# Subtracting the mean on ScalarE instead of VectorE in a banded-attention and MLP kernel, with two weight sums moved

## The chip, the cores and the metric

The kernel runs on one core of one Trainium2 chip. The metric is the device time of one execution in microseconds (us). Medians, with lowest and highest, are over all executions of a kernel that were timed. The profile is one traced execution. Its span is about 1.7 us shorter than the time that the same execution is given, so spans are compared with spans and times with times.

## The reference, cut to what matters

```python
# q, k, v: (8 batches, 8 heads, 576 positions, 64); window of 64 positions
scores = where(0 <= i - j < 64, q @ k.T / 8, -1e9)
x  = (softmax(scores) @ v).transpose(0, 2, 1, 3).reshape(8, 576, 512)
mu, var = mean(x), mean((x - mu) ** 2)              # of each row of 512
xn = (x - mu) / sqrt(var + 1e-6) * g_ln
out = x + relu(xn @ w_ch1) @ w_ch2                  # 512 -> 2048 -> 512
```

## The kernel before

Rows are worked in nine groups of 512, each of four blocks of 128 rows (`kb`). Groups 0 to 7 are the first 512 positions of each batch; group 8 collects the last 64 of all batches. For every block `b_step` multiplies scores by V, divides by the softmax sum, and takes mean and variance. `z_step` makes the f16 rows for the MLP, `zt_step` transposes them on TensorE and copies the result to `zT` on ScalarE. In groups 0 and 1 `z` is only `x - mean`; the division by the standard deviation is done at the end, in `add_out`, because ReLU lets a positive factor through.

```python
def b_step(g, kb):
    ...                                             # xps = attention product on TensorE
    nc.vector.reciprocal(out=rcp, in_=xps[:, :, D])                             # L323
    nc.vector.tensor_tensor(out=xn, in0=xps[:, :, 0:D], in1=rcp_b, op=ALU.mult) # L326
    nc.vector.bn_stats(out=stats, in_=xv)                                       # L328
    nc.vector.bn_aggr(out=mvg[g][:, kb, :], in_=stats)                          # L331
    if g < 2:
        z_step(g, kb)

def z_step(g, kb):
    z = p_blk.tile([128, DM], FP16, tag="z", ...)
    ...
    if g < 2:
        nc.vector.tensor_scalar(out=z, in0=xv, scalar1=mu, scalar2=None, op0=ALU.subtract)  # L341
        return
    ...                                             # groups 2 to 8: on GpSimd

def zt_step(g, kb, eng="act"):
    ...                                             # from group XZ on: a DMA transposes, most blocks
    for kc in range(NKC):
        nc.tensor.transpose(out=ztp[:, kc, :], in_=z[:, 128*kc:128*(kc+1)], identity=ident16)
    nc.scalar.copy(out=dst, in_=ztp)                # L363

def l1_half(half, i):                               # half a group of the first layer, two banks' worth
    ...                                             # matmuls hph (L531)
    nc.scalar.activation(out=hrT[...], in_=hps, func=AF.Relu, bias=0.0, scale=1.0)          # L536
```

A plan says in which slot of which group's MLP each of these steps is emitted. In program order the plan reads as follows (cut):

```python
zt_step(0, 0); vB_cur(0, 3, 0)
b_step(0, 2)                     # ends in z_step(0, 2)
zt_step(0, 1)                    # its copy gives zT to the first half of the first layer
s_mm(0, 3, True)                 # scores and exp of block 3
...
if g == 0:
    at(0, b_step, 0, 3); at(1, zt_step, 0, 2); at(3, zt_step, 0, 3); at(4, newton, 0, 0, 4)
    ...
    at(18, b_step, 1, 0); at(21, b_step, 1, 1); at(22, zt_step, 1, 0); at(24, zt_step, 1, 1)
    ...
    at(33, b_step, 1, 2)
if g == 1:
    ...
    at(1, b_step, 1, 3); at(2, zt_step, 1, 2); at(5, zt_step, 1, 3)
    at(25, w2_sums, 3, 0, 4); at(28, w2_sums, 3, 4, 8)     # T3 = b22 - b12
    ...
if g == 2:                                                 # T2 = T3 + b11, then T1 and T4
    for m, i in enumerate((2, 1, 4)):
        at(4 + 2*m, w2_sums, i, 0, 4); at(5 + 2*m, w2_sums, i, 4, 8)
```

The softmax here doesn't subtract the row's maximum and nothing guards it: scores larger than these inputs give would overflow.

## Time and profile before

| | before |
|---|---|
| time, median of the first three runs (lowest to highest) | 311.75 us (311.21 to 312.38) |
| profiled span | 310.4 us |
| mean granted TensorE clock | 0.998 |
| TensorE's last matmul ends / the output stores then take | 304.8 / 5.7 us |

The busy shares, the chain that ended last and the timelines of the start and of the seam between groups 0 and 1 are in the prediction.

### The profile page before, as it was taken

The page shows a single profiled execution, that of the slowest core. Times are in us where ns is not written, and L with a number is a line of the kernel's source. Part 1 is how long each engine was busy: PE and PEld are TensorE (multiplying, and loading weights), DVE is VectorE, ACT ScalarE, POOL GpSimd, SP SyncE. Part 2 cuts the span into 40 slices and gives each one's busy share as a digit, 9 for nine tenths or more (in the row PEclk, how much of TensorE's full clock was granted, in tenths as well). Part 3 has the DMA queues.
Part 4 walks back from the last instruction along what each step waited for, and adds up shares of the span by engine and source line. Part 5 has one row for each costly group of instructions (what it writes and reads, how often), then busy time and mean ns, then how long its engine had stood idle before and what let it go on. Part 6 is the DMA issues. An engine that isn't in the chain of part 4 may idle for free.

```text
span 310.4 us, 7624 instructions
## 1 busy us (share of the span) xinstructions
PE 297.7 (96%) x3089; PEld 197.6 (64%) x3089; DVE 222.0 (72%) x411; ACT 153.0 (49%) x258; POOL 172.2 (55%) x255
## 2 busy tenths in 40 slices
PE   7988998999999999999999999999999999999992
PEld 4556544597454468646964686459646855788882
DVE  0779585775775996589666965896569685777972
ACT  2586633487326742776247626762375048315500
POOL 6669676563871798279815983698246506204300
PEclk9999999999999999999999999999999999999999
DMA  8999999999766995899179997993690393003013
GB/s 193 259 385 291 334 356 278 291 297 185 163 166 193 255 196 116 259 298 138 35 224 309 202 159 219 312 146 66 205 179 19 52 203 137 2 0 137 0 37 101
DMA packets 109893, 57.43 MB, mean 185 GB/s; under 512 B 79841, under 2 KB 100833, under 8 KB 109858
## 3 DMA queue, kind: packets, MB, share of 16 engines
q1 hardware_dynamic: 108800, 53.75, 69.9%
q0 software_dynamic: 768, 2.80, 3.8%
q8 instruction: 24, 0.39, 0.5%
q10 hardware_dynamic: 290, 0.40, 0.4%
q14 instruction: 11, 0.09, 0.1%
HBM read 38.80 MB, written 9.44 MB: 155 GB/s over the span
## 4 chain that ended last, share of the span: by engine, by line
PE 81%; DVE 7%; SPq 4%; DMA 3%; ACT 1%; POOL 1%; issue 1%; POOLq 0%; ACTq 0%
PE hps L395 28%; PE pA L472 11%; PE pB L472 7%; PE pC L472 7%; PE hph L531 6%; PE ch L407 6%; PE xps L320 4%; PE sc L286 3%; DMA w1s<-in_moe_w_ch_dram 3%; PE tp L229 2%; PE lA L581 2%; SPq L141 2%; DVE sS L446 2%; PE ch L546 1%; SPq L89 1%; PE lC L581 1%
## 5 line engine op out<-in xcount | busy, mean ns | idle before, releaser
L395 PE MATMUL hps<-zT,w1g 128*128 128x512 f16 x416 | 96.3, 380 | 0.0
L399 ACT ACTIVATE hrT<-hps 128x512 f16<-128x512 f32 x104 | 62.4, 600 | 38.6 <-PE hps L395 35.0
L395 PEld LDWEIGHTS <-w1g 128*128 128x128 f16 x416 | 38.3, 98 | 41.9 <-issue 0.9
L293 ACT ACTIVATE pt<-sc 128x512 f16<-128x512 f32 x72 | 39.0, 595 | 27.8 <-DVE xn L479 15.6
L472 PEld LDWEIGHTS <-sS 128*128 128x128 f16 x448 | 43.3, 98 | 5.4 <-issue 0.5
L345 POOL TENSOR_SCALAR rsz<-mvg 128x1 f32<-128x1 f32 x28 | 10.3, 370 | 59.6 <-DVE mvg L331 58.6
L128 POOL CAST qk<-qk 128x1024 f16<-128x1024 f32 x32 | 35.6, 1128 | 13.7 <-DMA qk<-in_q_dram 8.3
L472 PEld LDWEIGHTS <-hrT 128*128 128x128 f16 x336 | 32.5, 98 | 5.3 <-ACT hrT L620 0.3
L215 ACT COPY qkT<-tp 128x1024 f16<-128x1024 f16 x16 | 16.1, 1012 | 35.9 <-PE tp L229 26.7
L300 DVE TENSOR_TENSOR pt<-pt,mask 128x1024 f16<-128x1024 f16 x32 | 25.6, 805 | 9.6 <-ACT pt L293 9.6
L479 DVE TENSOR_TENSOR xn<-pA,xn 128x512 f32<-128x512 f32 x28 | 19.2, 686 | 17.2 <-PE pA L472 17.2
L472 PE MATMUL pA<-wT,sS 128*128 128x256 f16 x224 | 26.9, 273 | 0.3 <-DVE xn L479 0.3
L348 POOL TENSOR_SCALAR z<-xn,rsz 128x512 f16<-128x512 f32 x28 | 25.3, 904 | 2.9
L472 PE MATMUL pC<-w2s,sS 128*128 128x256 f16 x224 | 26.9, 273 | 0.0
L323 DVE RECIPROCAL rcp<-xps 128x8 f32<-128x8 f32 x36 | 7.4, 205 | 26.1 <-PE xps L320 25.9
L328 DVE BATCH_NORM_STATS2 stats<-xn 128x6 f32<-128x512 f32 x36 | 25.0, 695 | 1.2
L326 DVE TENSOR_TENSOR xn<-xps,rcp 128x512 f32<-128x512 f32 x36 | 24.9, 691 | 1.2
L531 PE MATMUL hph<-zT,w1g 128*128 128x256 f16 x192 | 23.9, 273 | 1.8 <-ACT zT L363 1.1
L446 DVE TENSOR_TENSOR sS<-hrT 128x512 f16<-128x512 f16 (+1 forms) x40 | 24.5, 613 | 0.6 <-ACT hrT L399 0.6
L407 PE MATMUL ch<-w2s,hrT 128*128 128x512 f16 x96 | 22.9, 380 | 0.3 <-DVE xn L417 0.3
L531 PEld LDWEIGHTS <-w1g 128*128 128x128 f16 x192 | 17.9, 98 | 5.1 <-issue 1.5
L320 PEld LDWEIGHTS <-pt 128*64 128x64 f16 x576 | 12.2, 110 | 13.7 <-issue 5.9
(109 smaller groups left out, 454.1 us busy)
## 6 DMA issues: line engine op xcount, KB each, us to landing
out_dram<-xn SPq DMA_DIRECT2D x33, 256.0 KB, 2.7
qk<-in_q_dram SPq DMA_DIRECT2D x16, 512.0 KB, 6.4
qk<-in_k_dram SPq DMA_DIRECT2D x16, 512.0 KB, 7.4
v<-in_v_dram SPq DMA_DIRECT2D x32, 256.0 KB, 6.3
w2s<-in_moe_w_ch_dram SPq DMA_DIRECT2D x9, 512.0 KB, 9.0
w1s<-in_moe_w_ch_dram SPq DMA_DIRECT2D x4, 512.0 KB, 7.3
tk<-in_k_dram SPq DMA_DIRECT2D x8, 256.0 KB, 4.6
tv<-in_v_dram SPq DMA_DIRECT2D x8, 256.0 KB, 5.2
```

The costliest lines, as they stand in the source:

```text
L128: nc.gpsimd.tensor_copy(out=dst[:, :].rearrange("p (a j) e d -> p a e j d", j=j), in_=t[:, :].rearrange("p (a e j d) -> p a e j d", e=2, j ...
L293: nc.scalar.activation(out=o, in_=i, func=AF.Exp, bias=0.0, scale=scale)
L300: nc.vector.tensor_tensor(out=ptv, in0=ptv, in1=mb, op=ALU.mult)
L326: nc.vector.tensor_tensor(out=xn, in0=xps[:, :, 0:D], in1=rcp_b, op=ALU.mult)
L328: nc.vector.bn_stats(out=stats, in_=xv)
L348: nc.gpsimd.tensor_scalar(out=z, in0=xv, scalar1=rs, scalar2=nm, op0=ALU.mult, op1=ALU.add)
L395: nc.tensor.matmul(out=hps, lhsT=w1g[:, kc, 128 * hc:128 * (hc + 1)], rhs=zT[g][:, kc, :], start=(kc == 0), stop=(kc == NKC - 1),)
L399: nc.scalar.activation(out=hrT[:, hc, :], in_=hps, func=AF.Relu, bias=0.0, scale=1.0)
L407: nc.tensor.matmul(out=ch[kb], lhsT=hrT[:, hc, 128 * kb:128 * (kb + 1)], rhs=w2s[:, hc, :], start=(hc == 0), stop=(hc == NHC - 1),)
L446: nc.vector.tensor_tensor(out=o, in0=x, in1=y, op=op)
L472: nc.tensor.matmul(out=o, lhsT=a[:, c, 128 * p:128 * p + 128], rhs=wv[:, c, :], start=(first and (p == 0 or split_c) and c == 0), stop=(c ...
L531: nc.tensor.matmul(out=hps[:, e], lhsT=w1g[:, kc, 128 * hc:128 * (hc + 1)], rhs=zT[g][:, kc, 256 * half:256 * half + 256], start=(kc == 0) ...
```

## The change

Its intent is to take six of the eight subtractions of groups 0 and 1 off VectorE, where they collide with GpSimd's casts (the worst took 1885 ns instead of 486). ScalarE computes `Identity(x + bias)` with the bias minus the mean, which VectorE prepares as a 128x1 negation. The transpose of block 1 of group 1 comes one unit later, which gives `z` more time. The sum T3 of W2 comes earlier in group 1 and T2 takes its old slots there, a group sooner than before, which frees VectorE early in group 2. Whole diff:

```diff
@@ z_step
         if g < 2:
-            nc.vector.tensor_scalar(out=z, in0=xv, scalar1=mu, scalar2=None, op0=ALU.subtract)
+            if g == 0 and kb < 2:
+                nc.vector.tensor_scalar(out=z, in0=xv, scalar1=mu, scalar2=None, op0=ALU.subtract)
+            else:
+                nmu = p_blk.tile([128, 3], FP32, tag="rsz", name=f"nmu_{g}_{kb}")[:, 0:1]
+                nc.vector.tensor_scalar(out=nmu, in0=mu, scalar1=-1.0, scalar2=None, op0=ALU.mult)
+                nc.scalar.activation(out=z, in_=xv, func=AF.Identity, bias=nmu, scale=1.0)
             return
@@ plan, g == 0
-            at(24, zt_step, 1, 1)
+            at(25, zt_step, 1, 1)
@@ plan, g == 1
-            at(25, w2_sums, 3, 0, 4)
-            at(28, w2_sums, 3, 4, 8)
+            at(7, w2_sums, 3, 0, 4)
+            at(8, w2_sums, 3, 4, 8)
+            at(25, w2_sums, 2, 0, 4)
+            at(28, w2_sums, 2, 4, 8)
@@ plan, g == 2
-            for m, i in enumerate((2, 1, 4)):
+            for m, i in enumerate((1, 4)):
```

## The prediction

> **What bounds the kernel now.** I read the page first (busy shares, then the chain that ended last), then the timeline of single stretches, and in it the start of each matmul against the start of the one before.
>
> ```profile
> PE 297.7 (96%) x3089; PEld 197.6 (64%) x3089; DVE 222.0 (72%) x411; ACT 153.0 (49%) x258; POOL 172.2 (55%) x255
> PE 81%; DVE 7%; SPq 4%; DMA 3%; ACT 1%; POOL 1%; issue 1%; POOLq 0%; ACTq 0%
> ```
>
> TensorE is busy for 96%, and 81% of the chain that ended last is its own work. VectorE, which the change relieves, is 7% of it. Busy alone would not prove that TensorE has no slack, so I looked at the starts: from 26.7 us on, matmuls of 256 columns start every 0.11 us and those of 512 every 0.22. Larger holes than a normal change of weights are few: 0.2 us at 39.8, 0.2 at 46.3, 0.8 at 48.4, 0.4 at 49.1, 0.4 at 59.85, 0.5 at 116.0, 0.4 at 120.4, and none above 0.2 after that. So whatever TensorE loses before about 120 us reaches the end almost whole, and the most that this change can win is what it removes of those holes.
>
> The start, where blocks 2 and 3 of group 0 (rows in blocks of 128) are made (timeline, all engines; start, length, engine, line, tiles, idle before):
>
> ```profile
> 19.56 0.59 ACT L363 COPY zT<-ztp 128x512 f16<-128x512 f16 x1
> 20.04 1.09 ACT L293 ACTIVATE pt<-sc 128x512 f16<-128x512 f32 x2
> 20.20 1.27 PE L531 MATMUL hph<-zT,w1g 128*128 128x256 f16 x8 [0.21 <-ACT zT L363]
> 20.63 0.18 DVE L331 BATCH_NORM_AGGREGATE mvg<-stats 128x2 f32<-128x6 f32 x1
> 20.85 0.49 DVE L341 TENSOR_SCALAR z<-xn,mvg 128x512 f16<-128x512 f32 x1
> ...
> 23.58 0.18 DVE L331 BATCH_NORM_AGGREGATE mvg<-stats 128x2 f32<-128x6 f32 x1
> 25.58 0.60 ACT L536 ACTIVATE hrT<-hph 128x512 f16<-128x512 f32 x1 [0.28 <-PE hph L531]
> 26.08 0.58 ACT L363 COPY zT<-ztp 128x512 f16<-128x512 f16 x1
> 26.71 3.65 PE L531 MATMUL hph<-zT,w1g 128*128 128x256 f16 x32 [0.94 <-ACT zT L363]
> ```
>
> ScalarE copies zT of block 1 before the mean of block 2 exists (20.81), and TensorE starts the MLP at once.
>
> The seam between groups 0 and 1 (same view):
>
> ```profile
> 47.05 1.33 DVE L341 TENSOR_SCALAR z<-xn,mvg 128x512 f16<-128x512 f32 x1
> 47.06 1.04 POOL L128 CAST qk<-qk 128x1024 f16<-128x1024 f32 x1 [0.78 <-PE ch L546]
> 48.31 1.39 DVE L417 SCALAR_TENSOR_TENSOR xn<-ch,rstdg,xn 128x512 f32<-128x512 f32 x2
> 48.44 0.40 PE L360 MATMUL ztp<-ident,z 128*128 128x128 f16 x4 [0.65 <-DVE z L341]
> 49.10 1.89 PE L407 MATMUL ch<-w2s,hrT 128*128 128x512 f16 x8 [0.26 <-DVE xn L417]
> ...
> 59.71 0.60 ACT L536 ACTIVATE hrT<-hph 128x512 f16<-128x512 f32 x1 [2.12 <-PE hph L531]
> 61.20 1.05 PE L531 MATMUL hph<-zT,w1g 128*128 128x256 f16 x8
> 61.40 0.18 DVE L331 BATCH_NORM_AGGREGATE mvg<-stats 128x2 f32<-128x6 f32 x1
> ```
>
> At 47 us a 0.49 us subtraction takes 1.33 beside a GpSimd cast, and TensorE waits for it: this is what the change aims at. At 59.71 ScalarE empties the first hph bank before the mean of block 2 of group 1 exists (61.58).
>
> **What the Trainium skill says.** "SBUF — State Buffer", Who interferes with whom: VectorE's two-port operations (copy, cast, tensor_scalar) and GpSimd's instructions exclude each other for a whole instruction, while ScalarE waits for nobody. The trace agrees: the eight subtractions have a median of 486 ns and a maximum of 1885. It also shows that tiny ones are caught: the 128x4 steps of newton take 0.16 us alone and 0.63 beside GpSimd's w1 casts. "ScalarE: Activation LUTs", What ACT_TABLE_LOAD costs: an ACTIVATE with a pointer bias takes 280 ns + 0.833 ns per element, 707 ns for 512; the trace has no such row named, its ACTIVATEs of 512 take 600. I use 0.62 to 0.70. Both orders have one table load only, so Identity costs none. "TensorE: Matmul & The Clock Gate", Part 1: the array falls to half speed after an idle window of some 3.4 us. The trace shows two speeds at the start (transposes every 0.107 us until 8.7, then every 0.056).
>
> **The change part by part.** Built orders of both kernels show three moves.
>
> (a) Six subtractions (0.49 alone) leave VectorE; six 128x1 negations (0.16 alone, an estimate from newton's 128x4 rows) come, so 6 x 0.33 = 2.0 us less VectorE work. Six Identity passes, about 3.9 us, go to ScalarE, which is at 49%. Neither total bounds the kernel; what counts is that ScalarE works in order, and the new pass stands where the block step is written, in front of work that was ready earlier.
>
> Group 0, block 2: the pass comes ahead of the zT copy of block 1. Mean ready 20.81, negation to 21.01, pass 21.07 to 21.69, zT copy 21.6 to 22.2 (was 20.15), exps of block 3 to 23.2 (were 21.13). First hph at 22.25, 2.05 late. Block 3: attention product at 23.27 instead of 21.39; from there to its mean takes 2.37 us as before, so 25.64; the negation, in the middle of back-to-back casts, ends about 26.2; pass to 26.85. It stands before the ReLU of the second hph bank, which then ends at 27.4 and frees the bank of the fourth hph: 27.45 to 28.3; ReLU, then zT of block 3 to 29.5 (was 26.66). The second half of hph starts at 29.5 in place of 26.71: **+2.8 us**, less 0.2 because w2's last cast (46.28) is then no longer waited for.
>
> Group 1, blocks 0 and 1: ScalarE is idle from 41.7 to 46.3, so both passes fit. The wait for z goes, and the transpose a unit later gives it 0.86 us more. But the next matmul still needs the bank that the add at L417 frees, which runs after the mean of block 1 (47.02) and the negation: 48.0 to 48.7 by the clock of before, depending on whether a cast catches the negation. TensorE stood at 49.96 after that unit and the transpose; it will at 49.1 to 49.85. **-0.4 us**.
>
> Group 1, block 2: the pass now stands before the ReLU of the first hph. With TensorE 2.6 us later, GpSimd's casts of q and k at 56 to 58.6 are over when VectorE masks, so that mask is 0.7 shorter and 0.4 of hole at 59.85 goes. Mean at about 61.0, negation to 61.2, pass to 61.9, ReLU to 62.4: the third hph starts 62.45 instead of 61.20. Block 3: mean 63.1, pass to 63.95, ReLU of the third bank to 64.45, just in time. Sum **+1.3 us** (already net of the 0.4); if the cast of v catches this last negation it is up to 1.9 more.
>
> (b) T3 moves to the time after the qkT copies of group 1, where VectorE is idle for 3.0 us; T2 takes T3's old slots (same shape). So 2 x 0.68 us leave the stretch at 100 to 102 us of group 2, and the two halves of T4 move ahead of block 1's reciprocal. VectorE is full from 103 to 116, and TensorE waits at its end:
>
> ```profile
> 100.36 1.29 DVE L712 TENSOR_TENSOR wT<-wT,w2s 128x1024 f16<-128x1024 f16 x2
> 104.92 0.66 DVE L712 TENSOR_TENSOR wT<-w2s,wT 128x1024 f16<-128x1024 f16 x1
> 115.29 0.69 DVE L479 TENSOR_TENSOR xn<-pA,xn 128x512 f32<-128x512 f32 x1
> 116.03 1.91 PE L472 MATMUL pA<-wT,sS 128*128 128x256 f16 x16 [0.34 <-DVE xn L479]
> ```
>
> With some 1.3 us less in that stretch the hole of 0.5 closes, and perhaps part of the 0.4 at 120.4: **-0.6 us**.
>
> Sum: 2.8 - 0.2 - 0.4 + 1.3 - 0.6 = +2.9, so 311.75 + 2.9 = 314.6.
>
> **Rivals.** First, the change does what it is for: ScalarE has room, VectorE's collisions go, and the blocking is absorbed because the start waits for weights. Then only the gains stay, 0.4 + 0.4 + 0.6 and part of the 0.8, some 1.5 us: 310.2. For it speaks that the MLP waits for w1 casts at 23.28 and 23.95; against it that in my times the ReLU behind block 3's pass, not w1, is last by more than 3 us. Second, VectorE's negations are as exposed to GpSimd as the subtractions were, and each sits on the path to a ScalarE pass on which others queue: with the 1.9 of group 1 and another 0.5 in group 0 the time is 317. Third, TensorE's pauses at the start (2.3 us before the first hph, 1.7 before the fourth) come close enough to an idle window to drop its clock; some 3 us at half speed add 1.5 to 3 us: 316 to 318. The pauses of 0.9 us in the trace of before did not do so.
>
> **Range and chances.** My blocking terms follow from fixed orders and measured lengths; uncertain are the collisions with GpSimd, about 1.5 us either way, and whether I missed an absorption. 8 in 10: 311.0 to 317.5. Two per cent slower means over 318.0, which needs the second and third rivals together: 0.08. Two per cent faster means under 305.5, more than all holes after 26.7 us: 0.01.
>
> **What would show it.** First hph near 22.3 us and second half near 29.5; on ScalarE zT of block 1 after the pass; TensorE waiting for the ReLU at the third hph of group 1; no wait for z at the late transpose; the hole at 116 gone. If the second half starts before 27.5, the prediction is wrong by its main term; if it starts near 29.5 and the end is not later, something after it had slack that I did not see.

## More of the kernel before

One more view is useful for comparing: what TensorE itself waited for in the kernel before (columns: who waited for whom, us in total, times, the longest).

```profile
PE hph L531 <- ACT zT L363: 1.1, 2, 0.9
...
PE ztp L360 <- DVE z L341: 0.6, 1, 0.6
...
PE pA L472 <- DVE xn L479: 0.3, 1, 0.3
```

The whole list is some 6 us long in an execution of 310. The wait for `z` is the one that the change aims at; the wait of `pA` is the one that the moved sums may close.

## The result, and the profile after

| | before | after |
|---|---|---|
| time, median (lowest to highest), 6 runs each | 311.48 us (311.02 to 312.38) | 315.14 us (314.93 to 316.3) |
| ratio of the fast runs, 95% interval | | 1.0119 (1.0098 to 1.0141) |
| profiled span | 310.4 | 313.6 |
| mean granted TensorE clock | 0.998 | 0.989 |
| VectorE / ScalarE busy | 222.0 / 153.0 | 218.4 / 156.4 |

A ratio here and below is the mean time of one kernel's fast runs over that of the other's of the same rounds, so it is not quite the ratio of the medians that are quoted. Executions over 1.5% slower than the fastest of the same kernel are left out of the means. The changed kernel is 1.2% slower, well outside the scatter. The prediction was 314.6.

The line of the page on the chain that ended last, changed kernel:

```profile
PE 87%; ACT 5%; DVE 5%; issue 1%; POOL 0%; POOLq 0%; ACTq 0%
```

ScalarE went from 1% of that chain to 5%, VectorE from 7% to 5%. What TensorE waited for, changed kernel:

```profile
PE hph L536 <- ACT zT L368: 3.1, 2, 2.2
...
PE hph L536 <- ACT hrT L541: 1.5, 1, 1.5
```

Line numbers moved by up to five (L531 became L536). The waits for `z` and for the add before `pA` have left the list. In their place the wait of `hph` for the copy of `zT` grew from 1.1 to 3.1 us, and one of 1.5 us for a ReLU is new: both releasers are on ScalarE.

The start of group 0, changed kernel, timeline (start, length, engine, line, operation, idle before):

```profile
21.03 0.15 DVE L345 TENSOR_SCALAR nmu<-mvg 128x1 f32<-128x1 f32 x1
21.22 0.72 ACT L346 ACTIVATE z<-xn,nmu 128x512 f16<-128x512 f32 x1 [1.50 <-DVE nmu L345]
21.85 0.57 ACT L368 COPY zT<-ztp 128x512 f16<-128x512 f16 x1
22.46 1.15 PE L536 MATMUL hph<-zT,w1g 128*128 128x256 f16 x8 [2.19 <-ACT zT L368]
24.12 1.89 PE L536 MATMUL hph<-zT,w1g 128*128 128x256 f16 x8
26.34 0.72 ACT L346 ACTIVATE z<-xn,nmu 128x512 f16<-128x512 f32 x1 [2.09 <-DVE nmu L345]
26.96 0.58 ACT L541 ACTIVATE hrT<-hph 128x512 f16<-128x512 f32 x1
...
29.79 2.45 PE L536 MATMUL hph<-zT,w1g 128*128 128x256 f16 x21 [0.94 <-ACT zT L368]
```

The order on ScalarE: the pass for block 2 at 21.22, after an idle time of 1.50 us, and only then the copy of `zT` of block 1, which stood at 19.56 before. TensorE starts the MLP at 22.46 instead of 20.20. The same happens with block 3 at 26.34, ahead of a ReLU. The second half of `hph` starts at 29.79 instead of 26.71.

Block 2 of group 1, same view:

```profile
63.19 0.72 ACT L346 ACTIVATE z<-xn,nmu 128x512 f16<-128x512 f32 x1 [3.52 <-DVE nmu L345]
63.82 1.06 ACT L541 ACTIVATE hrT<-hph 128x512 f16<-128x512 f32 x2
64.45 1.03 PE L536 MATMUL hph<-zT,w1g 128*128 128x256 f16 x8 [1.50 <-ACT hrT L541]
```

ScalarE stood idle for 3.52 us in front of the pass, and the ReLU that would have emptied a bank stood behind it.

Following one and the same matmul through both traces gives the ledger, in us. Each row is the start of that matmul; the third column is the running difference, the fourth what the stretch since the row above added. (Both spans start 0.19 apart already at 17 us.)

| matmul | before | after | late by | added | predicted |
|---|---|---|---|---|---|
| first `hph` of group 0 | 20.20 | 22.46 | 2.26 | 2.07 | 2.05 |
| second half of `hph` | 26.71 | 29.79 | 3.08 | 0.82 | 0.75 |
| `ch` after the last cast of W2 | 46.34 | 49.37 | 3.03 | -0.05 | -0.2 |
| first layer's end, after the seam | 49.96 | 52.09 | 2.13 | -0.90 | -0.4 |
| third `hph` of group 1 | 61.20 | 64.45 | 3.25 | 1.12 | 1.3 with the rest of the stretch |
| `pA` with wT | 116.03 | 118.66 | 2.63 | -0.62 | -0.6 |
| end of TensorE | 304.79 | 307.41 | 2.62 | -0.01 | 0 |
| end of the span | 310.45 | 313.57 | 3.12 | 0.50 | 0 |

### The profile page after: what moved, and what is told of

It is laid out like the page before. It is cut to its first block, busy times and chain, and to the rows that moved or that the text cites. A ratio compares the mean times of both kernels' runs of the same rounds, so it can differ in the third digit from the quotient of the medians.

```text
span 313.6 us, 7634 instructions
## 1 busy us (share of the span) xinstructions
PE 298.2 (95%) x3089; PEld 199.1 (63%) x3089; DVE 218.4 (70%) x411; ACT 156.4 (50%) x264; POOL 171.1 (55%) x255
## 4 chain that ended last, share of the span: by engine, by line
PE 87%; ACT 5%; DVE 5%; issue 1%; POOL 0%; POOLq 0%; ACTq 0%
PE hps L400 30%; PE pA L477 12%; PE pB L477 8%; PE pC L477 8%; PE ch L412 6%; PE hph L536 6%; PE sc L286 4%; PE xps L320 4%; PE tp L229 3%; ACT pt L293 2%; PE lA L586 2%; PE warm L749 1%; DVE stats L328 1%; PE lC L586 1%; DVE xn L326 1%; ACT qkT L215 1%
## 5 line engine op out<-in xcount | busy, mean ns | idle before, releaser
L400 PEld LDWEIGHTS <-w1g 128*128 128x128 f16 x416 | 38.3, 98 | 42.0 <-issue 0.9
L300 DVE TENSOR_TENSOR pt<-pt,mask 128x1024 f16<-128x1024 f16 x32 | 26.6, 838 | 6.9 <-ACT pt L293 6.7
L536 PE MATMUL hph<-zT,w1g 128*128 128x256 f16 x192 | 24.6, 281 | 4.7 <-ACT zT L368 3.1
L536 PEld LDWEIGHTS <-w1g 128*128 128x128 f16 x192 | 18.6, 100 | 7.8 <-issue 2.8
```

Source lines behind the costliest of these rows:

```text
L300: nc.vector.tensor_tensor(out=ptv, in0=ptv, in1=mb, op=ALU.mult)
L400: nc.tensor.matmul(out=hps, lhsT=w1g[:, kc, 128 * hc:128 * (hc + 1)], rhs=zT[g][:, kc, :], start=(kc == 0), stop=(kc == NKC - 1),)
L536: nc.tensor.matmul(out=hps[:, e], lhsT=w1g[:, kc, 128 * hc:128 * (hc + 1)], rhs=zT[g][:, kc, 256 * half:256 * half + 256], start=(kc == 0) ...
```

## The experiments

Three theories were on trial. **Order**: ScalarE works in order, and the pass, which must wait for its mean, stands in front of work that is ready; what costs is the wait, not the work. **Work**: the passes themselves, or the longer path mean, negation, pass, cost the time. **Clock**: the pause of TensorE at the start dropped its clock. The last is not idle: in the timeline above, the eight matmuls at 24.12 took 1.89 us, which is half speed. Twelve kernels were run, in three calls; each call has its own runs of the kernel before on the same chip: 312.14 (310.68 to 315.6), 312.19 (311.0 to 312.92) and 311.68 (310.71 to 315.19), 11 runs each. All twelve gave correct results.

### a4_late_pass: the same passes, issued later

The changed kernel's instructions, with four of the six passes issued behind the work that is ready first. VectorE's order stays as it is.

```diff
-                nc.scalar.activation(out=z, in_=xv, func=AF.Identity, bias=nmu, scale=1.0)
+                late[(g, kb)] = (z, xv, nmu)      # z_pass(g, kb) issues the activation
+                if g == 1 and kb < 2:
+                    z_pass(g, kb)
...
 s_mm(0, 3, True)
+z_pass(0, 2)
...
 at(1, zt_step, 0, 2)
+at(1, z_pass, 0, 3)
...
+at(1, z_pass, 1, 2)       # group 1, before b_step(1, 3)
+at(3, z_pass, 1, 3)       # group 1
```

> The changed kernel with the same instructions, VectorE's order untouched; only four of the six ScalarE passes are issued later (group 0 block 2 after the exps of block 3, group 0 block 3 after the zT copy of block 2, group 1 block 2 after the second ReLU, group 1 block 3 after the fourth). Theory O (the loss is ready work of ScalarE standing behind a pass that waits for its mean): the 2.9 us of group 0 and the 1.1 us of group 1 go, the gains of the seam (0.9) and of the sums (0.5) stay: 310.1 us, 0.986 of the changed kernel. Rival W (the passes and negations cost by their work or by the longer path mean, negation, pass, transpose): nothing changes, 315 us. Rival C (the clock that fell to half between 24 and 26 us): nothing is changed in the cause either, unless the hole goes; then as O.

312.47 us (311.7 to 314.69), ratio 1.0023 (0.9983 to 1.0064): no longer distinguishable from the kernel before, though not the gain that I had expected. Timeline of this kernel at the start of group 0:

```profile
21.58 1.03 PE L544 MATMUL hph<-zT,w1g 128*128 128x256 f16 x8 [0.21 <-ACT zT L376]
...
22.42 0.72 ACT L361 ACTIVATE z<-xn,nmu 128x512 f16<-128x512 f32 x1
...
27.36 3.65 PE L544 MATMUL hph<-zT,w1g 128*128 128x256 f16 x32 [1.04 <-ACT zT L376]
```

The pass of 0.72 us is still there, but beside TensorE's work, and `hph` waits 0.21 us instead of 2.19. (This execution began 1.4 us late, hence 21.58; by 49 us that was made up.) At 116 us TensorE is 0.98 ahead of the kernel before. So in this trace the passes as work cost TensorE nothing. The end is another matter: the output stores took 6.31 us instead of 5.66 (see "Not foreseen" below), which takes back most of what TensorE won. Two of the six runs took 314.5 and 314.7; they were not traced and I cannot explain them, but runs like these occur in the kernel before too (314.18 and 315.6, the latter counted as slow).

### a5_tiny_read: the wait without the work

The kernel before, with the subtraction left on VectorE, plus a ScalarE instruction on one column that reads the mean at the place where the pass would stand. Its result is not used.

```diff
             nc.vector.tensor_scalar(out=z, in0=xv, scalar1=mu, ..., op0=ALU.subtract)
+            if not (g == 0 and kb < 2):
+                tiny = p_blk.tile([128, 3], FP32, tag="rsz", name=...)[:, 0:1]
+                nc.scalar.activation(out=tiny, in_=mu, func=AF.Identity, bias=0.0, scale=1.0)
```

> The kernel before, subtractions still on VectorE, no negations; at the place of each of the six passes ScalarE copies 128x1 of the mean into a scratch tile nobody reads. Theory O: the wait alone costs, so most of the loss appears without its work: mean of group 0 block 2 at 20.8, zT copy of block 1 to 21.7 instead of 20.15; second ReLU behind the mean of block 3; +1.3 us in group 0 and +1.2 in group 1: 314.0 us (1.008 of before). Rival W: six operations of 0.2 us on an engine half idle, within 0.3 us of before: 311.6.

314.88 us (313.91 to 317.29), ratio 1.0095 (1.0057 to 1.0133). Timeline of this kernel:

```profile
21.11 0.20 ACT L344 ACTIVATE tiny<-mvg 128x1 f32<-128x1 f32 x1 [1.31 <-DVE mvg L331]
21.22 0.57 ACT L366 COPY zT<-ztp 128x512 f16<-128x512 f16 x1
21.84 1.03 PE L534 MATMUL hph<-zT,w1g 128*128 128x256 f16 x8 [1.54 <-ACT zT L366]
```

Six instructions of 0.20 us, 1.2 us of work in all on an engine that is half idle, cost most of what the change cost. The copy that the MLP needs begins at 21.22, once the tiny read has had its mean, instead of 19.56. This refutes the theory of work and shows that the wait in the wrong place is enough. My sizes: +1.3 for group 0, and the trace has 1.43 (28.14 against 26.71); +1.2 for group 1, which was too large: TensorE comes to the first `hph` of group 1 already 1.46 late (60.03 against 58.57), is 1.92 late at the third (63.12 against 61.20) and 2.11 at its end (306.90 against 304.79), so that group 1 added some 0.65.

### a1_g0_vector and a2_seam_only: taking the passes back, part by part

```diff
-            if g == 0 and kb < 2:
+            if g == 0:                 # a1: group 0 back on VectorE
+            if g == 0 or kb > 1:       # a2: group 1's blocks 2 and 3 back as well
```

> The changed kernel with both rows blocks of group 0's second half subtracted on VectorE again; group 1 stays on ScalarE. Theory O: second half of hph near 26.9 us again, 2.9 us less: 312.3 us. Rival C (clock): the half speed at 24 us goes with the hole, the same number, but then a6 must gain as much. Rival W: a third of the loss (two passes of six) of 3.7 us: 313.9.

> The changed kernel with only the two blocks of group 1's first half on ScalarE (ScalarE is idle there), sums and late transpose as changed. Theory O: both losses go, both gains stay: 310.1 us, faster than before (311.5) by 0.4%. Rival W: 311.5 + 2/6 of the loss = 312.7. Against a4: if equal, moving the passes in the order is as good as not having them.

a1: 313.45 us (313.02 to 314.12), ratio 1.0042 (1.0013 to 1.0071). a2: 311.38 us (310.71 to 311.96), ratio 0.997 (0.9938 to 1.0002). From the changed kernel (1.0119) to a1 is 0.8%, or 2.4 us, for group 0's two passes; from a1 to a2 is 0.7%, or 2.2 us, for group 1's later two. I had predicted 2.6 and 1.3 for them. In the traces, too, group 1's share is larger: from the seam to the third `hph` of group 1 TensorE takes 12.77 us in a1 (49.81 to 62.58) and 10.93 in a2 (49.66 to 60.59), 1.84 apart. Of these, 1.36 are left at TensorE's end (305.58 against 304.22); the output stores then add 0.90 (6.70 us in a1, 5.80 in a2).

a2 missed my 310.1 by more than a microsecond: over the runs, the seam, on which it was to gain, brought nothing that can be told from what the sums bring alone (a3, below). Its timeline shows one thing that can hide such a gain; below it, in a fence of its own, that of b1, which has the code of the kernel before apart from one buffer more:

```profile
45.76 1.02 PE L551 MATMUL ch<-w2s,hrT 128*128 128x512 f16 x4 [0.39 <-POOL w2s L204]
```

```profile
47.62 0.75 DVE L341 TENSOR_SCALAR z<-xn,mvg 128x512 f16<-128x512 f32 x1
48.14 1.46 PE L546 MATMUL ch<-w2s,hrT 128*128 128x512 f16 x6 [0.51 <-POOL w2s L204]
```

In front of the seam TensorE waits for GpSimd to cast the last parts of W2, and these casts wait for their transfers, which arrive at a different time in each execution. The last matmul group that waits for a cast starts at 46.34 us in the profile of the kernel before, at 47.14 in a2, at 48.14 in b1. Where W2 is that late, `z` is ready in time even when VectorE makes it: in b1 the subtraction took only 0.75 us and TensorE passed the seam without a wait for it. So the hole of 0.65 us, on which the change was built, is not there in every execution. The changed kernel, 3 us late at this point, shows no wait for W2, and its seam is 0.9 shorter than that of the kernel before.

W2 alone does not explain why a2 is no better than a3, though. In the traces a2 comes to the second half of `hph` 0.48 us ahead of a3 and to the last group that waits for W2 0.31 behind: that much W2 took. But from this group to the end of the first layer after the seam, a2 takes 2.52 us (47.14 to 49.66) and a3 3.57 (46.83 to 50.40, with 0.60 of waiting for `z`). All ten kernels with the two passes take 2.51 to 2.88 there, the kernel before 3.62 and a5 4.03. So in the traces the seam does gain. a2 leaves it 0.74 ahead of a3 and is 0.03 behind by 94.73, where it waits 0.30 us for a DMA that transposes `z`: this gain was lost later. These are single traces; in the times, a2 (0.997) and a3 (0.9966), each known to about 0.3% and run on different chips, cannot be told apart.

### a3_sums_only: the moved sums alone

The kernel before with only the edit to the `w2_sums` slots.

> The kernel before with the sums T3 and T2 a period sooner and nothing else. Theory O: TensorE's hole of 0.5 us at 116 closes and nothing else moves: 0.998 of before, in the trace 0.5 us at that matmul and none ahead of it. Rival: the T3 sums collide with GpSimd's casts of q and k at 68 to 71 us and delay the mask of group 2 block 0, and nothing is won: 1.000.

310.97 us (310.14 to 311.72), ratio 0.9966 (0.9941 to 0.9991). This is the only kernel whose interval lies below 1. In its trace TensorE is 0.56 ahead at 116 us, as predicted for that step; the other half of the 1.06 us that the ratio makes I cannot place.

### a0_after and a6_keep_clock: the clock

a0 is the changed kernel once more, for the same chip. a6 fills TensorE's pause at the start with eight matmuls whose result is not used.

```diff
 s_mm(0, 3, True)
+keep_clock(8)
```

> The changed kernel once more, for a comparison on the same chip: 1.010 to 1.014 of before, with or without a fall of the clock near 24 us.

> The changed kernel with eight dummy matmuls of 512 columns (1.7 us) between the scores of group 0 block 3 and the first hph, where TensorE waits 2.2 us for the zT copy: the clock is not to fall at 24 us. Theory O: the attention product and second hph of group 0 run at full speed again, but the second ReLU still waits behind the pass of block 3; second half of hph at 29.4 in place of 29.8; 0.3 us less than a0_after. Rival C: the half clock is the loss; 2.5 us less than a0_after, at before.

a0: 316.37 us (315.31 to 318.1), ratio 1.0143 (1.011 to 1.0176), clock 0.984. a6: 316.42 us (314.91 to 318.12), ratio 1.0138 (1.0103 to 1.0173), clock 0.996. The timeline of a6, to set beside the line at 24.12 of the changed kernel:

```profile
22.54 1.03 PE L536 MATMUL hph<-zT,w1g 128*128 128x256 f16 x8 [0.46 <-ACT zT L368]
...
23.89 1.05 PE L536 MATMUL hph<-zT,w1g 128*128 128x256 f16 x8
```

Eight matmuls take 1.05 us instead of 1.89, so the drop of the clock is gone; the time is not. In the single traces the second half of `hph` starts 7.01 us after the first `hph` in a6, 7.33 in the changed kernel and 8.05 in a0, where half speed lasted 6.83 us instead of 3.41. So half speed moved that point by 0.3 and by 1.0 us, but over six runs nothing of it is left. The clocks of the single runs agree: the two executions of the changed kernel with the highest clock (0.997 and 0.996) still took 315.06 and 314.93 us, and all six of a6, with 0.994 to 0.997, took 314.91 or more. The clock did fall, as the third rival had it, and it is not what the change costs.

### a8_vector_g0_late_g1: the version that the parts suggested

a4 with group 0 on VectorE: nothing at the start is touched, the collision at the seam is avoided, group 1's later passes come late, the sums are moved.

```diff
-            if g == 0 and kb < 2:
+            if g == 0:
...
-z_pass(0, 2)
-at(1, z_pass, 0, 3)
```

> Group 0 on VectorE; group 1 on ScalarE with the passes of its second half issued after the second and the fourth ReLU; sums and transpose as changed. Theory O: all gains, no loss: 0.995 of before (310.0 us); the part won at the seam may be partly eaten by waits for w2's casts, as in a2_seam_only (1.0 us in three waits there), which the changed kernel hid by being late. If that is so, 0.997.

312.02 us (311.57 to 313.43), ratio 1.0007 (0.9982 to 1.0031): not the gain expected. TensorE is 1.14 ahead at 116 us (114.89 against 116.03), and then loses 1.7 at one place. Timeline:

```profile
182.89 0.76 POOL L355 TENSOR_SCALAR z<-xn,rsz 128x512 f16<-128x512 f32 x1 [2.06 <-DMA zT<-z]
183.71 0.40 PE L373 MATMUL ztp<-ident,z 128*128 128x128 f16 x4 [1.53 <-POOL z L355]
```

GpSimd may write this `z` only when the DMA that transposes the block before in the same buffer has read it, and in this trace that DMA did not come forward with TensorE (it was issued at 176.89, against 177.01 before). The profile is of the slowest run of a8 (313.43 us). In the trace of a4, with the same three buffers, the same `z` is written at 181.08 without such a wait, so it does not belong to every execution.

### b1_before_z4, b2_late_pass_z4, b3_g0v_late_z4: one more buffer for z

The kernel before, a4 and a8 with four buffers for `z`. To make room, the small tile `g1` shares another tile's buffer.

```diff
-        z = p_blk.tile([128, DM], FP16, tag="z", name=...)
+        z = p_blk.tile([128, DM], FP16, tag="z", name=..., bufs=4)
```

> The kernel before with a fourth buffer for z (its place in SBUF comes from the scaled-norm row g1, which moves into a buffer used later). Control: in before's trace no z waits for a transposing DMA, so the time stays, 1.000 of before, unless the slow ones among its runs (314 to 315.6) come from that wait; then the spread shrinks and the median stays.

> a4_late_pass (all the instructions of the changed kernel, passes late in ScalarE's order) with the fourth z buffer. If the two runs of a4_late_pass at 314.5 come from z waiting for the transposing DMA of the block three earlier (seen in the trace of a8: 2.06 us at 182.9), they go: median 311, 0.996 of before. If not, as a4: 1.002 with a spread of 3 us.

> a8_vector_g0_late_g1 with the fourth z buffer. Trace of a8: TensorE 1.1 us ahead of before at 116 us, 0.6 behind after the wait at 183. With the buffer the 1.1 us stay: 0.9965 of before, 311.1 us. If the wait only moves to the DMA queue (the transposed zT itself late), 1.000 as a8.

b1: 311.92 us (311.03 to 312.7), ratio 0.999 (0.9947 to 1.0034): the buffer alone does nothing, as expected of a control. b3: 312.04 us (311.58 to 312.83), ratio 0.9995 (0.9953 to 1.0037). The wait at 183 is gone and TensorE ends at 303.60, 1.2 ahead of the kernel before, but the output stores after it take 6.71 us instead of 5.66, and the span is 310.3 again. b2: 311.78 us (311.41 to 314.26), ratio 0.9985 (0.994 to 1.0031); I had expected its spread to shrink, and it did not. Its profile fell on the slowest run and shows a wait that no other trace here has:

```profile
69.41 0.74 POOL L165 DMA_DIRECT2D vB<-vA  x1 [0.30 <-POOL vA L147]
...
70.94 3.00 POOL L128 CAST qk<-qk 128x1024 f16<-128x1024 f32 x3
71.49 3.01 DVE L300 TENSOR_TENSOR pt<-pt,mask 128x1024 f16<-128x1024 f16 x1 [1.23 <-ACT pt L293]
...
77.64 0.19 PE L320 MATMUL xps<-vB,pt 128*64 128x65 f16 x1 [2.42 <-DMA vB<-vA]
```

TensorE waited 2.42 us for a DMA that copies rows of V into `vB`. GpSimd issues it behind its cast of V, at 69.41 here and at 65.84 to 69.18 in the other traces, where no attention product waits for it. The 2.42 us account for this one run, which is 2.5 us above the median. A mask of 0.69 us also took 3.01, behind three casts of GpSimd that followed one another without a gap; but it ended at 74.50, 3 us before TensorE went on, and is not what TensorE waited for. Whether the other single slow runs, in the kernel before too, have the same cause stays open: none of them was traced.

### a7_transpose_24: the transpose back at its place

a2 with `at(24, zt_step, 1, 1)` as in the kernel before.

> a2_seam_only with the transpose of group 1 block 1 back a unit earlier, after unit 24. The ScalarE pass of that block ends near 49.1 us in a2, while TensorE reaches this place at 48.6: it waits 0.5 to 0.6 us for z, and the bank for the next unit is free by then: 0.5 us more than a2_seam_only, 0.999 of before. If the bank of the add is what holds TensorE anyway, no difference, 0.997.

311.24 us (310.36 to 315.32, the last counted as slow), ratio 0.9969 (0.992 to 1.0017): no different from a2. TensorE waits only 0.22 us for `z` in the trace, because the mean and the negation came a microsecond earlier than I had reckoned. With the pass on ScalarE, the later transpose is worth nothing that can be measured; my expectation of half a microsecond was wrong.

## Why the prediction was right or wrong

The time (315.14 for 314.6) and the mechanism were right, and every one of the four parts had the right sign in the trace. That the time came out so close is partly luck: the difference forecast was 2.9 us and the measured one is 3.7, and in the trace the seam gained 0.5 more than forecast while the end lost 0.5 that nobody had foreseen. Put in the order in which experiments add them, the ratios to the kernel before are:

| kernel | ratio | what the step adds | in us of 312 | predicted |
|---|---|---|---|---|
| a3: sums only | 0.9966 | sums | -1.1 | -0.6 |
| a2: and the seam | 0.997 | blocks 0 and 1 of group 1 | +0.1 | -0.4 |
| a1: and the rest of group 1 | 1.0042 | blocks 2 and 3 of group 1 | +2.2 | +1.3 |
| changed kernel, first time / a0 | 1.0119 / 1.0143 | blocks 2 and 3 of group 0 | +2.4 / +3.2 | +2.6 |

The intervals are 0.4 to 0.7% wide, so single steps are known to no better than about a microsecond. The kernels were not all on one chip. Two sizes were off without bearing on the result: VectorE's busy time fell by 3.6 us instead of 2.0, and the passes took 0.72 us each instead of 0.62 to 0.70.

**Group 0, "+2.8 us".** Right, and to the tenth in the trace: 2.89. It came out because the order on ScalarE was read from the built program and the lengths from the trace. The Trainium skill, "PSUM — Partial Sum Buffer", Engine vs sequencer instructions, calls the queues of ScalarE, VectorE and GpSimd strictly first in, first out. The traces agree: in a5 ScalarE stood idle for 1.31 us before a read of 0.20, and the copy behind it, which runs at 19.56 in the kernel before, came at 21.22. The subtraction of 0.2 for the cast of W2 was too large: 0.05 was absorbed.

**The seam, "-0.4 us".** The step that failed is the sentence that the add "runs after the mean of block 1 (47.02) and the negation: 48.0 to 48.7 by the clock of before, depending on whether a cast catches the negation". The timeline of the changed kernel at this place:

```profile
48.08 1.04 POOL L128 CAST qk<-qk 128x1024 f16<-128x1024 f32 x1 [0.83 <-PE xps L320]
48.16 0.15 DVE L345 TENSOR_SCALAR nmu<-mvg 128x1 f32<-128x1 f32 x1
...
51.01 1.02 PE L412 MATMUL ch<-w2s,hrT 128*128 128x512 f16 x4 [0.18 <-DVE xn L422]
```

The negation starts inside a cast that lasts until 49.12, and takes 0.15 us all the same. A view by tile of the subtractions before and of the negations after (count, shortest, median and longest in ns, first and last start) says that it took no longer in any of the six, of which four (at 21.03, 26.15, 48.16 and 50.14) ran wholly inside a GpSimd instruction and two met none; first before, then after:

```profile
L341 DVE TENSOR_SCALAR z<-xn,mvg x8: 486/486/1885, 15.0 to 63.9; 128x512 f16<-128x512 f32 x8
```

```profile
L345 DVE TENSOR_SCALAR nmu<-mvg x6: 153/153/154, 21.0 to 64.9; 128x1 f32<-128x1 f32 x6
```

I had taken newton's 128x4 steps, which do suffer (0.16 and 0.63), as the model for 128x1. So the seam gained 0.9 in the changed kernel, not 0.4. Over the runs the gain does not show: a2 is no better than a3, and in its trace what the seam gave was lost again by 95 us. The prediction also took the arrival of W2 from one trace (its 0.2 us) for fixed; in b1 W2 came so late that there was no hole at the seam to close.

**Group 1, "+1.3 us".** The mechanism was right, with the ReLU behind the pass, and the size in the trace is close: 1.1 at the third `hph`. That includes the hole of 0.4 at 59.85, which closes in the changed kernel. (It is closed in a3 too, 59.01 to 59.90 for 58.57 to 59.85 from the first `hph` to the second, and a3 has the code of the kernel before up to there; so it comes and goes without the change.) In a2 the hole is closed as well (its stretch to the third `hph` is 10.93 us, that of the kernel before 11.24), so the step from a2 to a1 has to be held against 1.3 + 0.4 = 1.7; the traces give 1.84 at the third `hph` and 1.36 at TensorE's end, and the times 2.2, with the stores at the end in them.

**The sums, "-0.6 us".** Right in the trace of the changed kernel (0.62) and in a3's (0.56). The hole at 120.4 stayed, as allowed for.

**The rivals.** The first, all blocking absorbed, is refuted by the 3.08 us at the second half of `hph`. The second, negations caught by GpSimd, did not occur, though four of the six ran beside a GpSimd instruction. The third did occur, with 3.41 us at half speed, which cost about 0.3 us there and not 1.5 to 3; a6 shows that it did not set the time.

**Not foreseen.** The stores at the end took 6.16 us in the changed kernel instead of 5.66, which is half a microsecond of the 3.1. All kernels have the same code there, but this is not scatter. One line of the page goes with it, that of a DMA queue which the page calls "instruction" (packets, MB, share), first before, then after:

```profile
q14 instruction: 11, 0.09, 0.1%
```

```profile
q14 instruction: 12, 0.10, 0.1%
```

In the five traces with 11 packets (the kernel before, a3, b1, a2 and a7, which add no instruction or two to ScalarE) the stores take 5.64 to 5.80 us; in the nine with 12 (four or six instructions more) they take 6.14 to 6.71. In these nine the last packet of that queue starts 3.5 to 4.3 us after TensorE's end, inside the span. So four or more further instructions on ScalarE go with 0.5 to 1.0 us at the end, wherever in the queue they stand; the tail takes back 0.65 of the 0.99 us that TensorE wins in a4, and 1.05 of the 1.19 in b3. This is one trace of each kernel; why is not shown, and no experiment aimed at it.

## What to carry to other kernels

Moving an operation to an engine with room is not free when that engine works in order: ask what stands behind it in the queue while it waits for its operand, not how busy the engine is. Write the instruction where its operand is ready, behind whatever is ready sooner; here that alone took the loss from 1.2 or 1.4% to one that cannot be told from zero, though not to a gain. And look for a wait in more than one trace before building on it: the hole at the seam is in the profile of the kernel before and not in b1's, and a gain in the middle can be lost again at a later wait or at the end.

## What the Trainium skill lacked or had wrong

- "SBUF — State Buffer", Who interferes with whom, lists tensor_scalar among the operations that can take the ports shared with GpSimd, and leaves the conditions to "VectorE: DVE Perf Modes", Mode 2×_2P, where the operand is split along a dimension that is not of size one. Neither says what follows for tiny operands: an f32 tensor_scalar of 128x1 was not caught in any of the four that ran wholly inside a GpSimd instruction (153 to 154 ns, one in the cast at 48.08), while ones of 128x4 took 0.16 us alone and up to 0.67 beside GpSimd's work.
- The first of these sections also says that whoever issues first has the shared ports for a whole instruction while the other is blocked. In b2 a VectorE tensor_tensor took 3.01 us instead of 0.69, across three casts in a row; that a wait can outlast one instruction isn't said.
- "TensorE: Matmul & The Clock Gate", Part 1, gives an idle window of some 3.4 us that runs freely, and tells without a figure of a kernel whose short pauses made the clock swing. In the changed kernel the clock fell to half at 23.25 us (eight matmuls of 256 columns then took 1.89 us instead of 1.05), though TensorE had stood idle for only 2.19 of the 3.4 us before; in a5 a wait of 1.54 us was not followed by it. Filling part of the wait with eight matmuls, which left 0.46, kept full speed. How much of a window must be idle isn't on the page.
- No page that I read gives the cost of a wait at the head of a queue that works in order. Here six reads of 0.20 us, put where their operand was not ready, cost 0.95%.
